# Threshold attention and a low-rank mixer on one core: weight copies and casts of the first five pairs on other engines, and another opening

## The chip, the core and the metric

The kernel runs on one core of a Trainium2 chip. A core has TensorE (PE: matmuls and transposes, with its weight loads shown as PEld), VectorE (DVE), ScalarE (ACT), GpSimd (POOL) and SyncE (SP, which here only issues DMAs). PE writes to PSUM, eight banks of 2 KB in each of 128 partitions; the other tiles lie in SBUF. DMAs are issued here by SP, ACT and POOL. Each engine works through its own instructions in the order in which the program gives them, and semaphores make it wait for the others.

The metric is the device time of one execution in microseconds, the median over runs. Before the change it is 692.33 us (three runs, 691.79 to 692.9).

## The reference

Eight batches of eight heads, 576 positions, 64 columns a head. Attention keeps only the scores that are within tau = 0.02 of their row's largest; its result, 512 columns a position, goes through a mixer of low rank over the positions and a two-layer network over the columns.

```python
scores = scale * np.matmul(q, k.transpose(0, 1, 3, 2))
thresh = np.max(scores, axis=-1, keepdims=True) - tau
scores = np.where(scores >= thresh, scores, -1000000000.0)
attn = np.exp(scores - np.max(scores, axis=-1, keepdims=True))
attn = attn / (np.sum(attn, axis=-1, keepdims=True) + 1e-09)
x = np.matmul(attn, v)                       # then (8, 576, 512)
...
h = x.transpose(0, 2, 1) @ U @ V
u = x + h.transpose(0, 2, 1)
out = u + np.maximum(u @ w_ch1, 0.0) @ w_ch2
```

## The kernel before

The work is cut into 32 pairs of heads, four to a batch. Of a pair, q and k (fp32) are loaded into qkraw, with head 0 and head 1 side by side, and transposed on PE into qkT: `turn_main` for q, `turn_main` for k (four 128x128 transposes each) and `turn_rest` for the last half tiles of both (L625, L638), each followed by a copy on ACT (L631, L644). A pair has 576 rows, which is four and a half tiles of 128; the half tiles of two neighbouring pairs share one step, so two pairs have nine steps. Pairs 0, 2, 4 and so on own the shared step, i = 4.

A step does, for both heads x = 0, 1: scores on PE into a trio of PSUM banks (L696); a copy to SBUF on DVE that also takes the row's extreme (`weigh`, L725, into s_sb and m); the threshold on POOL (L742, into thr); the exponential on ACT (L748, into e_sb); the selection on DVE, which multiplies the exponential by "is over the threshold" and gives the row sum (L755, reads s_sb and e_sb, writes w_ring); a small copy on POOL that doubles the last 64 columns (L766); five transposes on PE (L773); and a copy of these from PSUM to wT_ring or wT4 (`copy_w`, L781). That last copy is on ACT for x = 0 and on DVE for x = 1: `COPIED = (SCA, VEC)`.

`value_tasks` then multiplies the transposed weights by v (L835 to L843), divides by the sums (POOL, L874 for the first four pairs and L901 later), makes a bf16 copy xb of the result (`narrow`, two casts on ACT, L906 and L907), takes it through U and V on PE (L914, L929), adds on DVE (L936), makes a second bf16 copy ub (`narrow_u`, ACT, L943), and transposes that for the network (L951, L959). v itself is split into a high part (`top`, a cast on POOL, L667) and a low part (L660). When the four pairs of a batch are done, `mixer_tasks` runs the two layers on PE (L1024 and L1040 up, L1057 down), spread between the attention steps of later batches. The attention and the mixer of different batches thus lie beside each other, except at the start, where there is no finished batch, and at the end.

The order of all this is written out. Every function call is a `Task` with an engine, a cost, what it depends on and the PSUM banks it needs. A planner outside the kernel has made from them the tuple `ORDER`, which lists the 3,879 tasks in the order in which their instructions are issued to the engines' queues, and `BANK`, which gives the PSUM bank of each. Negative numbers in `ORDER` are `fill` tasks: one matmul on identb into a given bank (L526), without a use for its result. The costs and the due times `DUE` are not read when the kernel is built. `Order.run` walks through the tuple and calls the tasks.

For the opening, the loads of pair 0 go out on three queues: q on SP (three DMAs) and POOL (one), k on ACT (three) and POOL (one). Each is one head's rows of one half of the partitions. The first six pairs after it are loaded by SP alone (`LOADERS`), which also loads v (L587) and sends the outputs; later pairs are loaded by POOL.

Of the kernel before, what the change touches and what calls it, by code (L numbers as in the profile page):

```python
# [68 lines left out]
P = 128  # L69
# [18 lines left out]
COPIED = (SCA, VEC)  # L88
PHASES = (1, 2, 3, 4, 5, 6, 8, 28)
# [4 lines left out]
HIGH = 32  # L94
# [20 lines left out]
class Task:  # L115
# [17 lines left out]
    24, 21, 26, 25, 19, 22, 23, 20, 1, 47, 0, 27, 45, 28, 44, 41, -1, -1, -1, -1, -1, -1, 32, 2, 34, 30, 46, 33, 35,  # L133
    31, 29, 48, -2, -2, 59, 43, 49, 61, 42, 60, 68, 39, -3, -3, -3, -3, -3, 73, 63, 62, 3, 69, 40, 74, 228, 70, 36,
    -8, -8, -8, 71, 75, 225, 77, 87, 64, 224, 56, 82, 72, 226, 89, 37, 227, -6, 52, 76, 88, 57, 50, 53, 231, 78,
    101, 4, 96, 83, 51, 90, 54, 102, 84, 55, 248, 65, 91, 38, 103, -8, -8, 85, 244, 115, 86, 110, 104, 92, 233, 79,
    105, 246, 117, 93, 58, 229, -3, -3, 94, 116, 80, 66, 249, 97, 81, 235, 130, 230, 67, 106, 95, 251, 111, 188,
    124, 247, 132, 112, 236, 118, 232, 98, 131, 107, 119, 245, -7, 108, 125, 189, 113, 99, 252, 109, 144, 120, 139,
    234, 100, 121, 250, 237, 126, 114, 5, 145, 122, 238, 191, 133, 146, 134, 140, 127, 153, 147, 239, 158, 128, 397,
    123, 141, 135, 192, 194, 240, 160, 148, 136, 142, 159, 241, 213, 149, 172, 214, 6, 195, 154, 167, 259, 150, 143,  # L140
    137, 161, 260, 257, 242, 174, 186, 138, 155, 243, 173, 258, -8, 156, 255, 162, 187, 157, 264, 175, 523, 181,
    168, 521, 256, 163, 169, 526, 266, 190, 151, 393, 265, 193, 152, 527, 196, 279, 7, 197, -7, -7, -7, -7, 207,
    402, 182, 164, 273, 524, 278, 267, 198, 176, 183, 396, 165, 274, 184, 166, 170, 129, 185, 275, 199, 280, 268,
    171, 399, -5, -5, 276, 177, 286, 291, 253, 269, 281, 178, 394, 277, 208, 8, 254, 282, 270, 179, 395, 205, 292,
    283, 200, 180, 525, 206, 293, 398, 210, 287, 300, 294, 400, 201, 288, 284, 392, 211, 261, 305, 289, 202, 271,
    306, 295, 262, 290, 272, 307, 296, 308, 318, 301, 313, 309, 285, 302, 319, 203, 297, 212, 405, 320, 204, 263,
    322, 333, 298, 406, 303, 209, 334, 407, 327, 375, 321, 314, 310, 299, 304, 315, 403, 341, 9, 328, 316, 376, 698,
    311, 215, 317, 408, 336, 335, 522, 323, -6, -6, 346, 404, 342, 332, 312, 337, 216, 699, 347, 373, 338, 694, 329,
    217, 324, 348, 343, 350, 401, 330, 360, 218, 349, 528, 344, 325, 361, 529, 363, 339, 378, 374, 695, 326, 362,
    331, 377, 345, 340, 520, 10, 364, 381, 355, 697, 412, 351, 368, 700, 356, 379, 696, 382, 380, 413, 530, 352,  # L150
    365, 414, 383, 693, -8, 531, 416, 409, 353, 426, 384, 369, 415, 354, -8, -8, 219, 535, 385, 427, 532, 370, 366,
    410, 421, 371, 220, 357, 533, 536, 417, 386, 447, 221, 367, 372, 418, 222, 422, 358, 534, 419, 223, 387, 359,
    423, 420, 11, 388, -5, 424, 429, 428, 425, 540, 439, 430, 389, 448, 440, 434, 431, 411, 541, 432, 542, 390, 719,
    441, 391, 554, 543, 544, 713, 555, 444, 449, 442, 545, 549, 567, 435, 433, 537, 445, 550, 562, 556, 569, 546,
    557, 12, 704, 568, 547, 446, 705, 706, 582, 551, 436, 570, 707, 581, 443, 437, 548, 708, 717, 438, 576, 558, -5,
    552, 715, 595, 709, 571, 563, 866, 450, 864, 577, 584, 13, 596, 451, 559, 553, 564, 452, 583, 589, 597, 871,
    565, 453, 560, 566, 720, 454, 561, 716, 458, 572, 455, 870, 604, 459, 598, -4, -4, -4, 456, 14, 651, 609, 457,
    599, 610, 464, 585, 622, 590, 612, 600, 465, 591, 623, 573, 460, 578, 611, 624, 538, 626, 601, 466, 539, 617,
    637, 461, 579, 636, 574, 714, 721, 467, 462, 605, 625, 575, 594, 580, 468, 868, 463, 618, 702, 733, 701, 469,
    627, 631, 723, 613, 652, 722, 632, 639, 703, 592, 734, 644, 633, 606, 586, 593, 619, 649, 15, 737, 470, 747,  # L160
    718, 735, 587, 471, 602, 638, 724, 628, 653, 588, 736, 748, 865, 607, 472, 725, 869, 608, 603, 640, 474, 749,
    473, 645, 614, 760, 475, 738, 671, 750, 739, 755, 761, 620, 742, 762, 615, 476, 616, 775, 763, 646, 764, 478,
    641, 774, 634, 743, 479, 642, 486, 477, 635, 744, 769, 621, 728, 726, 751, 643, 480, 1013, 756, 729, 487, 647,
    867, 481, 629, 770, 482, 1014, 630, 765, 776, 727, 659, 648, 483, 766, 484, 771, 672, 752, 777, 1015, 787, 485,
    16, 778, 660, 782, 1020, 661, 650, 757, 788, 1019, 655, 789, 779, 791, 1016, 740, 803, 790, 656, 745, 710, 741,
    681, 746, 753, 802, 682, 772, 662, 796, 780, 657, 673, 804, 781, 683, 654, 773, 754, 658, 792, 767, 877, 674,
    17, 768, 879, 758, 675, 711, 875, 880, 805, 759, 677, 783, 1186, 878, 676, 876, 797, 488, 678, 730, 810, 815,
    679, 663, 811, 1188, 842, 489, 684, 680, 816, 490, 18, 829, 712, 664, 817, 492, 665, 819, 1192, 830, 666, 491,
    493, 1018, 806, 685, 844, 831, 667, 832, 818, 812, 798, 784, 824, 494, 807, 731, 837, 793, 825, 686, 1017, 813,
    687, 794, 820, 1187, 668, 808, 785, 795, 826, 495, 814, 821, 809, 786, 833, 827, 845, 822, 496, 669, 838, 799,  # L170
    834, 670, 848, 843, 823, 839, 800, 732, 846, 835, 849, 828, 688, 836, 840, 850, 497, 1022, 841, -6, 884, 689,
    801, 1191, 690, 1021, 847, 872, 1189, 885, 1028, 874, 1024, 886, 1029, 1023, 1026, 1025, 898, 887, 873, 852,
    1212, 1027, 899, 691, 851, 921, 853, 888, 854, 855, 922, 1033, 893, 889, 1190, 692, 1211, 923, 894, 1209, 1034,
    499, 900, 890, 881, 1047, 1037, 500, 906, 1035, 895, 882, 891, 911, 1048, 896, 1193, 892, 913, 897, 1036, 901,
    907, 1060, 856, 902, 908, 914, 1042, 915, 1213, 912, 1050, 1062, 903, 501, 1208, 1055, 1061, 916, 857, 1038,
    1206, 909, 858, 904, 502, 910, 1049, 905, 1039, 1210, 1043, 859, 1040, 883, 503, 860, 917, 1069, 1075, 861,
    1207, 506, 1194, 1074, 918, 1030, 1041, 1195, 862, 919, 1199, 1051, 863, 1197, 924, 1200, 1056, 507, 1052, 1064,
    1088, 1077, 1057, 1063, 1076, 1065, 1082, 920, 1198, 1090, 508, 1066, 925, 1031, 1089, 1032, 1201, 1103, 1053,
    1202, 509, 1054, 1102, 1044, 1216, 1091, 1045, 1083, 498, 926, 1058, 927, 1070, 1067, 510, 513, 1110, 1215,
    1059, 1071, 1084, 1046, 928, 1104, 1068, 1214, 514, 929, 1097, 1196, 1078, 1072, 1092, 1115, 1073, 1087, 930,  # L180
    1093, 1105, 1094, 1116, 504, 933, 515, 934, 1117, 516, 935, 1111, 1118, 1085, 517, 931, 936, 1086, 1079, 932,
    1359, 1129, 937, 1080, 1144, 1130, 1081, 1098, 1119, 1095, 1226, 1145, 1106, 1137, 1120, 1107, 1096, 1146, 1124,
    1131, 1227, 938, 518, 1132, 1228, 1217, 1099, 1112, 939, 1138, 1363, 1100, 1221, 1148, 1125, 1360, 1222, 1218,
    1121, 1133, 1229, 1113, 1149, 940, 1235, 1114, 1362, 1101, 1142, 1152, 1358, 1241, 941, 1219, 1230, 1139, 1143,
    1126, 1174, 1236, 1220, 1108, 970, 1240, 1175, 1153, 1248, 1150, 1242, 944, 1109, 1176, 1492, 1231, 971, 1361,
    942, 1154, 1243, 1249, 1237, 1253, 1164, 945, 1357, 1165, 943, 1151, 1232, 1254, 1134, 1127, 1255, 1257, 1122,
    946, 1267, 1256, 1123, 1147, 1128, 1135, 511, 947, 1233, 1268, 1140, 1136, 1238, 1141, 1203, 1234, 948, 1258,
    1262, 1280, 1244, 1364, 1275, 1239, 1155, 1270, 1245, 1263, 1250, 949, 1281, 1166, 1204, 1156, 1205, 1295, 1157,
    1282, 1167, 950, 1264, 1158, 1284, 1269, 1168, 1283, 1246, 1296, 1177, 951, 1159, 1251, 1247, 1271, 1170, 1252,
    1368, 1160, 1171, 1223, 972, 1172, 1161, 1285, 1308, 1488, 973, 1276, 1297, 1369, 1298, 1277, 1173, 1309, 1289,  # L190
# [233 lines left out]
def kernel(  # L424
# [127 lines left out]
    def load_tasks(p, pr):  # L552
# [5 lines left out]
        def one(kind, e, part, to, of, j, deps):  # L558
# [6 lines left out]
            def first(_):  # L565
# [3 lines left out]
                       dma=0.6 if p == 0 and e != POOL else 0.4)  # L569

        lo, hi = slice(0, HB), slice(HB, P)
        loads = {"q": [], "k": [], "v": []}

        by = {"S": SP, "A": SCA, "P": POOL}
        eq, ek, eq3, ek3 = (SP, SCA, POOL, POOL) if p == 0 else \
# [642 lines left out]
```

## Time and profile before

| | us | share of the span |
|---|---|---|
| Median of three runs | 692.33 | |
| The profiled execution, its time | 691.71 | |
| The profiled execution, its span | 689.9 | 100% |
| PE busy | 652.5 | 95% |
| DVE busy | 554.8 | 80% |
| ACT busy | 521.9 | 76% |
| POOL busy | 453.8 | 66% |

The costliest groups, one row each: busy time and mean duration, then how long the engine was idle just before such an instruction and what ended most of that.

```profile
L755 DVE SCALAR_TENSOR_TENSOR w_ring<-s_sb,thr,e_sb 128x576 bf16<-128x576 f32 x288 | 242.0, 863 | 17.9 <-POOL thr L742 5.0
L748 ACT ACTIVATE e_sb<-s_sb,m 128x576 bf16<-128x576 f32 x288 | 217.6, 778 | 36.8 <-DVE s_sb L725 27.7
L725 DVE TENSOR_SCALAR_CACHE_REDUCE s_sb<-trio 128x576 f32<-128x576 f32 x288 | 205.7, 750 | 22.5 <-PE trio L696 18.2
L766 POOL COPY w_ring<-w_ring 128x64 bf16<-128x64 bf16 x288 | 89.6, 328 | 84.4 <-DVE w_ring L755 74.9
```

The granted clock of PE is at full speed in all forty slices of the span. The page's busy time of PE is that of pipelined matmuls whose ends are modelled, so 95% is not PE at its peak. Durations of neighbouring rows on DVE and ACT overlap by some tens of nanoseconds, so the cost of an instruction is read from the distance between two starts where they stand back to back. The share of an engine is a mean over stretches of different kinds; tables by stretch of time say more.

### The profile page before, as it was taken

What the parts mean: (1) busy time and instruction counts of PE and PEld (TensorE: products, weight loads), DVE (VectorE), ACT (ScalarE), POOL (GpSimd) and SP (SyncE); (2) the same over time, 40 slices, a digit from 0 to 9 for tenths busy, and PEclk for the clock granted to TensorE, in tenths of its full rate; (3) what the DMA queues carried; (4) which work ended last, traced back from release to release, by engine and by line L of the source; (5) the groups of instructions that cost most, each with busy time, mean ns of one, the idle gap of its engine ahead of it and who ended that gap; (6) DMA issues with size and microseconds to landing.
All of it is one profiled execution on the core that took longest, in us unless ns stands there. A gap on an engine that the chain in (4) does not pass through costs nothing.

```text
span 689.9 us, 19776 instructions
## 1 busy us (share of the span) xinstructions
PE 652.5 (95%) x7537; PEld 425.6 (62%) x7619; DVE 554.8 (80%) x1469; ACT 521.9 (76%) x1001; POOL 453.8 (66%) x887
## 2 busy tenths in 40 slices
PE   7988899999998999999999999999999999999997
PEld 3655655666666656566667667665666667656543
DVE  5999899889999998997889898899886987772102
ACT  3778779878888968878778788688877886767440
POOL 6566576887688786867887887788567665444020
PEclk9999999999999999999999999999999999999999
DMA  8664252422103132131122213323021321110223
GB/s 146 118 122 90 43 107 66 78 77 66 34 24 94 34 89 59 43 97 41 56 65 60 68 44 97 79 62 86 22 59 41 94 55 24 30 32 2 47 46 77
DMA packets 49503, 44.41 MB, mean 64 GB/s; under 512 B 28672, under 2 KB 40528, under 8 KB 49408
## 3 DMA queue, kind: packets, MB, share of 16 engines
q1 hardware_dynamic: 36320, 23.58, 14.5%
q0 software_dynamic: 12128, 19.22, 12.4%
q8 instruction: 60, 0.98, 0.6%
q10 hardware_dynamic: 960, 0.34, 0.2%
q14 instruction: 35, 0.29, 0.1%
HBM read 37.90 MB, written 9.44 MB: 69 GB/s over the span
## 4 chain that ended last, share of the span: by engine, by line
PE 57%; DVE 16%; ACT 7%; POOL 7%; issue 7%; DMA 4%; SPq 2%; another core or an unknown queue 0%; POOLq 0%; DVEq 0%; ACTq 0%
PE trio L696 12%; DVE w_ring L755 8%; PE trio L1057 8%; PE trio L1024 7%; DVE s_sb L725 6%; PE bank L1057 5%; PE bank L1024 5%; PE trio L773 4%; PE bank L839 3%; PE trio L839 3%; PE bank L773 3%; ACT e_sb L748 3%; POOL qkraw L563 2%; DVE wT_ring L781 2%; POOL x L901 1%
## 5 line engine op out<-in xcount | busy, mean ns | idle before, releaser
L755 DVE SCALAR_TENSOR_TENSOR w_ring<-s_sb,thr,e_sb 128x576 bf16<-128x576 f32 x288 | 242.0, 863 | 17.9 <-POOL thr L742 5.0
L748 ACT ACTIVATE e_sb<-s_sb,m 128x576 bf16<-128x576 f32 x288 | 217.6, 778 | 36.8 <-DVE s_sb L725 27.7
L725 DVE TENSOR_SCALAR_CACHE_REDUCE s_sb<-trio 128x576 f32<-128x576 f32 x288 | 205.7, 750 | 22.5 <-PE trio L696 18.2
L696 PE MATMUL trio<-qkT 64*64 64x288 f32 (+2 forms) x2304 | 160.1, 409 | 3.5 <-DVE wT_ring L781 1.3
L766 POOL COPY w_ring<-w_ring 128x64 bf16<-128x64 bf16 x288 | 89.6, 328 | 84.4 <-DVE w_ring L755 74.9
L773 PEld LDWEIGHTS <-w_ring 128*128 128x128 bf16 x1440 | 91.6, 98 | 48.7 <-issue 15.8
L696 PEld LDWEIGHTS trio<-qkT 64*64 64x64 f32 x2304 | 83.4, 132 | 52.1 <-issue 6.4
L1057 PEld LDWEIGHTS <-R 128*128 128x128 bf16 x576 | 52.6, 98 | 52.9 <-issue 5.6
L773 PE MATMUL trio<-identb,w_ring 128*128 128x128 bf16 x855 | 71.2, 219 | 6.3 <-DVE s_sb L725 3.1
L901 POOL TENSOR_TENSOR x<-x,rec 128x256 f32<-128x256 f32 (+1 forms) x84 | 51.9, 621 | 37.7 <-DVE x L894 33.2
L1024 PEld LDWEIGHTS <-W1b 128*128 128x128 bf16 x512 | 45.6, 98 | 49.2 <-issue 5.8
L563 POOL DMA_DIRECT2D qkraw<-in_q_dram x101 | 67.4, 668 | 9.5 <-PE bank L625 5.5
L742 POOL TENSOR_SCALAR thr<-m 128x2 f32<-128x2 f32 x144 | 44.5, 309 | 43.0 <-DVE s_sb L725 33.6
L1057 PE MATMUL bank<-W2b,R 128*128 128x512 bf16 x268 | 68.3, 379 | 1.8 <-issue 0.5
L563 POOL DMA_DIRECT2D qkraw<-in_k_dram x101 | 67.4, 668 | 3.8 <-issue 2.1
L1057 PE MATMUL trio<-W2b,R 128*128 128x512 bf16 x271 | 68.3, 379 | 1.4 <-ACT R L1014 0.7
L1024 PE MATMUL trio<-uT,W1b 128*128 128x512 bf16 x246 | 62.1, 379 | 3.2 <-DVE s_sb L725 2.3
L1024 PE MATMUL bank<-uT,W1b 128*128 128x512 bf16 x223 | 61.1, 379 | 1.3
L1014 ACT ACTIVATE R<-trio 128x512 bf16<-128x512 f32 x74 | 43.6, 602 | 23.7 <-PE trio L1024 16.8
L839 PEld LDWEIGHTS <-wT_ring 128*128 128x128 bf16 x896 | 55.0, 98 | 7.6 <-issue 4.9
L660 POOL TENSOR_TENSOR vh<-vraw_ring,vh 64x128 bf16<-64x128 f32 (+1 forms) x64 | 54.5, 852 | 2.8
L773 PE MATMUL bank<-identb,w_ring 128*128 128x128 bf16 x585 | 51.1, 219 | 4.1 <-DVE x L936 1.3
(116 smaller groups left out, 1025.3 us busy)
## 6 DMA issues: line engine op xcount, KB each, us to landing
out_dram<-o SPq DMA_DIRECT2D x71, 128.0 KB, 2.4
vraw_ring<-in_v_dram SPq DMA_DIRECT2D x32, 160.0 KB, 3.4
vraw_ring<-in_v_dram SPq DMA_DIRECT2D x32, 128.0 KB, 3.2
qkraw<-in_k_dram POOLq DMA_DIRECT2D x51, 80.0 KB, 2.5
qkraw<-in_q_dram POOLq DMA_DIRECT2D x50, 80.0 KB, 2.7
qkraw<-in_q_dram POOLq DMA_DIRECT2D x51, 64.0 KB, 2.4
qkraw<-in_k_dram POOLq DMA_DIRECT2D x50, 64.0 KB, 2.4
W1b<-in_moe_w_ch_dram POOLq DMA_DIRECT2D x8, 256.0 KB, 4.5
```

What stands on the lines that cost most here:

```text
L563: queue.dma_start(pr.qkraw[part, to, j, :], src[:, j, of, :])
L660: nc.gpsimd.tensor_tensor(out=pr.vh[part, tiles_, :, h, :], in0=raw[part, tiles_], in1=pr.vh[part, tiles_, :, 0, :], op=ALU.subtract)
L696: mm = nc.tensor.matmul(cols[part, lo:hi], a.tT[hs, 0, rows], a.tT[hs, 1, lo:hi], start=True, stop=True)
L725: nc.vector.tensor_scalar(out=s_sb, in0=score_cols(slot, x), scalar1=-scale, scalar2=None, op0=ALU.mult, op1=ALU.min, accum_out=m[:, x:x + 1])
L748: nc.scalar.activation(out=e_sb, in_=s_sb, func=ACT.Exp, bias=m[:, x:x + 1], scale=-1.0)
L755: nc.vector.scalar_tensor_tensor(out=w_sb[:, 0:S], in0=s_sb, scalar=thr_[:, x:x + 1], in1=e_sb, op0=ALU.is_le, op1=ALU.mult, accum_out=pr. ...
L766: nc.gpsimd.tensor_copy(out=w_sb[:, x, S:640], in_=w_sb[:, x, 512:S])
L773: nc.tensor.transpose(ps[:, kt * P:(kt + 1) * P], w_sb[:, kt * P:(kt + 1) * P], identb)
L839: nc.tensor.matmul(av[:, 2 * a + j, :], w, pr.vh[:, kt, j, :, :], start=kt == 0, stop=False)
L901: nc.gpsimd.tensor_tensor(out=x, in0=x, in1=over_sum(part), op=ALU.mult)
L1024: nc.tensor.matmul(bank[t.got[0]], W1b[:, dt, ft * P:(ft + 1) * P], bt.uT[:, dt, :], start=(dt == 0), stop=(dt == 3))
L1057: nc.tensor.matmul(ch, R2[:, ft, lo:lo + P], W2b[:, ft, :], start=(ft == 0), stop=(ft == 15))
```

## The change

It has five parts. Line numbers in the text are those of the kernel before.

First, `FRONT = 5`: in the first five pairs, `copy_w` goes to ACT for both heads in the steps i = 0, 2, 4. For x = 1 that takes 13 copies from DVE. Second, in the same pairs, the casts of `narrow` and `narrow_u` go from ACT to POOL. Third, the opening. For pair 0, k comes first: each half of the partitions is loaded by ACT (head 0) and SP (head 1). q's tile 0 comes apart, by two small loads on POOL, and q's half tile by a load on ACT; q's other tiles are loaded after k, on SP. k is transposed in two tasks of two tiles, one copied by ACT and one by DVE; q's tile 0 is transposed alone and copied by DVE. The first score step waits for q's tile 0, k and the half tiles, and no longer for the rest of q. Fourth, two costs are written differently (`top` 0.72 for 1.1, `copy_w` on DVE 0.404 for 0.42). Fifth, `ORDER` and `BANK` are new throughout, with 3,886 tasks and 23 `fill` entries instead of 43.

```diff
+FRONT = 5
...
 ORDER = (
...
-        for j in range(2):
-            loads["q"].append(one("q", eq, lo, slice(0, 5), slice(0, 5), j, freed))
-            loads["q"].append(one("q", eq3 if j or p else eq, hi, slice(0, 4), slice(5, 9), j, freed))
...
+            k_ = [opening("k", SCA, lo, slice(5, 9), slice(0, 4), one_, 0.5),
+                  opening("k", SP, lo, slice(5, 9), slice(0, 4), two_, 0.5)]
+            k_ += [opening("k", SCA, hi, slice(4, 9), slice(4, 9), one_, 0.6),
+                   opening("k", SP, hi, slice(4, 9), slice(4, 9), two_, 0.6)]
+            loads["q0"] = [opening("q", POOL, lo, one_, one_, both, 0.25),
+                           opening("q", POOL, hi, one_, slice(5, 6), both, 0.25),
+                           opening("q", SCA, lo, slice(4, 5), slice(4, 5), both, 0.25)]
+            loads["k"] = k_
+            for j, e in ((one_, SP), (two_, SP)):
+                loads["q"].append(opening("q", e, lo, slice(1, 4), slice(1, 4), j, 0.4))
+                loads["q"].append(opening("q", e, hi, slice(1, 4), slice(6, 9), j, 0.4))
...
+                def copy_k(_):
+                    nc.scalar.copy(out=pr.tT[:, 1, 0:256], in_=bank[halves[0].got[0]][:, 0:256])
+
+                def copy_k2(_):
+                    nc.vector.tensor_copy(out=pr.tT[:, 1, 256:512], in_=bank[halves[1].got[0]][:, 0:256])
...
+            def copy_q0(_):
+                nc.vector.tensor_copy(out=pr.tT[:, 0, 0:P], in_=bank[q0.got[0]][:, 0:P])
...
-                for name in ("qT", "kT", "qk4T")]
+                for name in (("q0T" if (p, i) == (0, 0) else "qT"), "kT0", "kT", "qk4T")]
...
+            mover = SCA if p < FRONT and i % 2 == 0 else COPIED[x]
...
-            t = add(COPIED[x], 0.42 if COPIED[x] == VEC else 0.575, copy_w, [t], frees=[t])
+            t = add(mover, 0.404 if mover == VEC else 0.575, copy_w, [t], frees=[t])
...
+        front = p < FRONT
+        copy = nc.gpsimd.tensor_copy if front else nc.scalar.copy
...
-            nc.scalar.copy(out=pr.xb[:, 0:4, :], in_=bt.x[:, :, pr.cols])
-            nc.scalar.copy(out=pr.xb[bt.h4, 4, :], in_=bt.x4[bt.h4, pr.cols])
+            copy(out=pr.xb[:, 0:4, :], in_=bt.x[:, :, pr.cols])
+            copy(out=pr.xb[bt.h4, 4, :], in_=bt.x4[bt.h4, pr.cols])
...
-            nc.scalar.copy(out=pr.ub, in_=bt.x[:, :, pr.cols])
+            copy(out=pr.ub, in_=bt.x[:, :, pr.cols])
```

## The prediction

> **What bounds the kernel now.** I read the page's busy times and slices first, then the same by stretches, then what VectorE (DVE) waits for.
>
> ```profile
> PE 652.5 (95%) x7537; PEld 425.6 (62%) x7619; DVE 554.8 (80%) x1469; ACT 521.9 (76%) x1001; POOL 453.8 (66%) x887
> ...
> PE   7988899999998999999999999999999999999997
> ...
> DVE  5999899889999998997889898899886987772102
> ACT  3778779878888968878778788688877886767440
> ```
>
> By the first row TensorE (PE) is the bound at 95%. That is an average. In the slices (17.2 us each) PE is below nine tenths in four of the first six, where DVE mostly shows 9; from there on PE is full, and DVE falls away at the end. The windows sharpen it (per engine: busy us and instructions):
>
> ```profile
> 28.00:68.00 40.00, 35.67 (x589) 24.69 (x587) 39.34 (x110) 31.64 (x62) 25.31 (x58) 1.00 0.54 98
> 68.00:80.00 12.00, 8.72 (x145) 6.97 (x146) 9.07 (x25) 8.69 (x20) 5.35 (x14) 1.00 0.39 63
> 80.00:112.00 32.00, 28.88 (x358) 17.86 (x359) 31.30 (x86) 26.82 (x49) 24.09 (x50) 1.00 0.45 90
> 112.00:135.00 23.00, 22.51 (x268) 15.45 (x270) 20.63 (x58) 19.95 (x40) 18.60 (x36) 1.00 0.35 62
> ```
>
> The third busy column is DVE: 39.3 of 40 us, a gap at 68 to 80, 31.3 of 32, and only after 112 us is PE the fuller one (22.5 of 23). So there are two regimes: up to about 112 us, which is where the first five pairs are worked on, DVE sets the pace, and PE fills part of its time with warm-up matmuls (L526: 39 of 43 stand in the order before the 20th of the 77 score tasks). Afterwards PE does. In 10 to 112 us DVE waits for this:
>
> ```profile
> DVE s_sb L725 <- PE trio L696: 7.7, 5, 6.7
> DVE wT_ring L781 <- ACT wT_ring L781: 1.6, 2, 1.2
> DVE x L936 <- PE trio L929: 1.4, 1, 1.4
> DVE rec L810 <- ACT rec L807: 0.6, 1, 0.6
> DVE w_ring L755 <- POOL thr L742: 0.3, 1, 0.3
> ```
>
> 6.7 of the first row is the start of the kernel itself. What is left is some 5 us in 102: an instruction taken from DVE here is worth nearly its length. In 112 to 560 us it would be worth little by itself.
>
> **The change, part by part.**
>
> *1. Thirteen copies of transposed weights leave DVE for ScalarE (ACT).* Pairs 0, 2, 4 have tiles 0, 2, 4 and pairs 1, 3 have tiles 0, 2 for which the second copy moves: 3x3 + 2x2 = 13. The rows of the two engines (min/median/max ns):
>
> ```profile
> L781 ACT COPY wT_ring<-trio x71: 669/692/755, 22.4 to 628.0; 128x640 bf16<-128x640 bf16 x71
> ...
> L781 DVE COPY wT_ring<-trio x78: 427/485/493, 14.8 to 628.7; 128x640 bf16<-128x640 bf16 x78
> ```
>
> Rows overlap on an engine. On the timeline a DVE copy starts at 42.49 and the next one at 42.89: it costs 0.40, not 0.485. Two ACT copies in a row at 23.00 take 1.29 together: 0.60 each. So DVE gives up 13 x 0.40 = **5.2 us**, and ACT takes on 13 x 0.60 = 7.8 us.
>
> *2. Casts of the first five pairs leave ACT for GpSimd (POOL).* xb is two casts on ACT (medians 618 and 296 ns), ub one (618); less 0.1 overlap each, about 0.72 + 0.52 = 1.24 us a pair, 6.2 us in five. ACT's balance is 7.8 - 6.2 = +1.6 us on the 79.6 us that it is busy in 10 to 112 us; in a front of about 97 us that is 84%. ACT's largest idle there is 7.5 us in which its exponentials (L748) wait for DVE's score row (L725), and no wait of a DVE select (L755) for an exponential is in the list. So I cost ACT at nothing: its idle, and DVE being late itself, hide it. Without that cover the price is rival B. Its lower end is a gain, the 1.6 us of DVE waits for ACT copies, since fewer copies on DVE must follow one on ACT.
>
> POOL has no such cast before. Nearest rows: L667, a cast fp32 to bf16 of 640 columns, median 720 ns, and L766, 64 columns, 238 ns. That is (720 - 238)/576 = 0.84 ns a column, so 0.61 us for 512 columns and 0.29 for 128: xb 0.90, ub 0.61, and 5 x 1.51 = 7.6 us on POOL. POOL is busy 54.8 of 84 us in 28 to 112; with 7.6 more in some 79 us it is at 79%. Behind a cast stand POOL's thresholds (L742) and twin copies (L766), for which DVE and PE wait; today DVE waits 0.3 us for them in the front, which is why I cost the queueing at nothing, with up to 0.6 a cast, 9 us, if each met a threshold that is due. As xb and ub lead to the mixer of batch 0 only through PE work that has the pairs' transposes and scores beside it, their extra 0.1 us each is hidden; uncovered it would be 5 x 0.2 = 1 us.
>
> Here a rule speaks against the change. The Trainium skill (SBUF — State Buffer, Who interferes with whom) says that a VectorE instruction with two SBUF inputs contends with a GpSimd instruction that reads SBUF, and that the later of the two stands fully blocked until the first ends. L755 is such an instruction (s_sb and e_sb), the casts read SBUF. By the rule at its worst each of the 15 casts holds a select for its whole length: 7.6 us, more than the change brings. The rows are far milder. L755 means 863 ns over the kernel and 825 in 10 to 112 us, against 814 for an undisturbed one (its median); 288 x 49 ns = 14.1 us lost, beside 180.7 us of POOL's larger SBUF readers (L660 54.5, L901 51.9, L1076 40.9, L667 26.5, L874 6.8). That is 0.08 us lost for each us of such work, so 7.6 us cost **+0.6**. The ends are 0 and 7.6; I take the row's value. It fits the rule's mechanism, not its worst case.
>
> *3. The opening.* Before, the first score matmuls start 2.6 us after the first transposes (page time 6.02), and DVE starts 1.4 us after that:
>
> ```profile
> 6.05 1.09 PE L625 MATMUL trio<-ident,qkraw 128*128 128x128 f32 x4
> ...
> 7.18 0.59 ACT L631 COPY qkT<-trio 128x512 f32<-128x512 f32 x1 [4.20 <-PE trio L625]
> ...
> 8.62 1.20 PE L696 MATMUL trio<-qkT 64*64 64x288 f32 x16 [0.24 <-ACT qkT L631]
> ```
>
> Nine transposes and three copies in a row on ACT (0.59, 0.27, 0.59) lie in those 2.6 us. Afterwards six transposes come first (q's tile 0, k's four, the shared one) and two engines copy. From the rows: six weight loads at some 0.16, 0.3 until PE's result is out, the last DVE copy about 0.36 (half the columns of a 0.59 ACT copy, for which L870 with 256 columns shows 0.37), 0.1 of hand-over: 1.7 us. That saves 0.9. But the transposes may start later: q's tile 0 comes by POOL's second load, which before was issued at 2.51 and took 3.9 us to land (6.4), against 6.02 now. Net about **-0.6**; ends -1.6 (all of k and q0 there at 5.0) and +0.4. The two copies that DVE gains lie before its first score row, in idle time. A skill rule bears on loading k by two queues: DMA: Bandwidth & Descriptors (Issuing engines are not separate DMA queues) says that several issuing engines only save the issue time. By it the second queue is worth one issue, about 0.7 us in SP's rows; I counted less, since SP's own loads of q now wait behind k's.
>
> SP issues six loads of pair 0 instead of three, but pair 1's values move behind pair 1's q and k: both orders reach pair 1's last load as their 17th issue, at about 12 us. It landed at 16.7, and PE waited 0.6 us for it with the fourth score step queued behind; now that step stands ahead of pair 1's transposes. I count nothing for it.
>
> *4. The whole order and the banks are new.* All 3,886 tasks are re-planned. Counted at equal score tasks, the work ahead of them on PE is within about 1 us of before for most, on DVE 4 to 5 us less from the 16th on. Twenty fillers fall away (43 to 23), 20 x 0.216 = 4.3 us of PE time that stood in waiting; they are the same microseconds and are not added. All remaining costs are equal, so past the front the whole schedule should stand earlier by what the front gained, because PE, full from there on, does the same work from an earlier start.
>
> **Sum.** Span 689.9 - 5.2 + 0.6 - 0.6 = 684.7. The profiled execution took 691.71, 1.8 more than its span, so 686.5. The median of the three runs, 692.33, is 0.6 above that execution: **687.1 us**, 0.75% below. I allow 0.4 for new places where PE waits and say **687.5**.
>
> **The rivals.**
>
> *A. The loads pace the front (no change).* In 62 to 70 us the chain of waits leaves DVE: SP issues values and q/k loads in its fixed order, and the last lands at 70.05:
>
> ```profile
> 62.60 0.55 SPq L587
> 63.20 0.60 SPq L587
> 63.84 1.71 SPq L563
> 65.60 4.31 DMA qkraw<-in_q_dram
> 70.05 0.63 PE bank L625 x4
> ```
>
> If this and later loads hold at their times, DVE's 5.2 us turn into a longer gap at 68 to 80. Against it: SP's loads wait for buffers that earlier work frees, so they move with it. Only some 1 us of opening and later copies would be left: 691.5.
>
> *B. ACT's queue becomes the bound (slower).* Each moved copy waits on PE's transposes, and behind it on ACT's fixed order stand the exponentials, behind these DVE's selects. If each of the 13 delays a select by its own 0.60, that is 7.8 us: 687.5 + 7.8 = 695.3. It decides from (692.3 - 687.5)/13 = 0.37 us a copy. For it: ACT's copies already wait 2.8 us for PE in this stretch. Against it: the idle of ACT above.
>
> *C. The waits of the front go too.* PE waits 3.1 us for qkraw, DVE 1.6 for ACT copies; a better order removes most: 687.5 - 4 = 683.5.
>
> **How the numbers follow.** Forecast 0.52 (685.5 to 690.5, its own range), C 0.18, A 0.13, B 0.17. This kernel's runs can tell about 0.2%, 1.4 us, from nothing. Faster: forecast, C and a little of A, 0.72; same: most of A and of the weaker B, 0.11; slower: 0.17. The range goes from C's 683.5 to 694.0, which takes in part of B and the 7.6 us of port contention up to about 6.
>
> **What would show it.** Right: first scores at about 8.0, 131 DVE copies at L781's successor and 157 on ACT, DVE's busy time in the front still 97% while the score row of the 57th tile (105.8 us now) starts 4 to 6 us earlier, selects there still near 830 ns, and the same distance kept to the end. Wrong: DVE gaps that end at ACT's exponentials (B), PE waits for qkraw grown by several us (A), selects over 900 ns in the front (port), or a lead at 110 us that is gone at 600 (the new order).

## The result, and the profile after

The changed kernel takes 689.8 us (median of ten runs, 689.34 to 690.45); the kernel before, run beside it, takes 691.98 us. The ratio is 0.9967, with a 95% interval from 0.9959 to 0.9976. So it is faster, by 0.33%: the sign and the range of the forecast hold, and the size is less than half of the 4.8 us that were forecast. The profiled execution took 689.98 us with a span of 688.2 us; before it was 689.9 us, so the span lost 1.7 us.

The page of the kernel after, with the same rows as were shown of before (busy us, share of the span, instructions; then busy tenths in 40 slices of 17.2 us), and three of its costliest groups (busy us, mean ns, idle before and what ended it):

```profile
PE 651.1 (95%) x7516; PEld 424.2 (62%) x7599; DVE 562.7 (82%) x1458; ACT 525.7 (76%) x999; POOL 463.0 (67%) x902
...
PE   7988889899999999999999999999998999999997
...
DVE  5999998799999999898899899799888997854001
ACT  3988788777998868987778888878877787767540
...
L818 DVE SCALAR_TENSOR_TENSOR w_ring<-s_sb,thr,e_sb 128x576 bf16<-128x576 f32 x288 | 255.4, 905 | 25.0 <-ACT e_sb L811 10.9
L811 ACT ACTIVATE e_sb<-s_sb,m 128x576 bf16<-128x576 f32 x288 | 216.7, 778 | 30.5 <-DVE w_ring L818 18.3
L788 DVE TENSOR_SCALAR_CACHE_REDUCE s_sb<-trio 128x576 f32<-128x576 f32 x288 | 206.5, 749 | 18.8 <-PE trio L759 13.2
```

Three things are to be seen. DVE has thirteen copies less and is yet busy 7.9 us longer (562.7 for 554.8). The reason stands in the first group, L818, the select that was L755: its mean went from 863 to 905 ns, 12.1 us over the 288. And PE has one new slice below nine tenths far behind the front, the 31st, which covers 516 to 533 us.

The windows of after, over the same stretches as before (us, then busy us of PE, PEld, DVE, ACT and POOL, each with its instructions):

```profile
28.00:68.00 40.00, 36.07 (x608) 25.62 (x603) 39.46 (x110) 35.24 (x67) 29.18 (x64) 1.00 0.55 108
68.00:80.00 12.00, 10.76 (x200) 7.92 (x200) 11.50 (x28) 9.75 (x20) 9.20 (x18) 1.00 0.37 62
80.00:112.00 32.00, 29.30 (x311) 17.23 (x313) 31.76 (x87) 27.44 (x50) 26.39 (x56) 1.00 0.39 80
112.00:135.00 23.00, 21.55 (x273) 14.30 (x275) 18.54 (x49) 16.43 (x32) 18.86 (x36) 1.00 0.40 79
```

and what DVE waits for in 10 to 112 us (us in total, times, longest):

```profile
DVE s_sb L788 <- PE trio L759: 3.0, 2, 2.5
DVE w_ring L818 <- POOL thr L805: 1.2, 3, 0.5
DVE w_ring L818 <- ACT e_sb L811: 0.5, 1, 0.5
```

DVE still paces the front, and the gap at 68 to 80 us is closed. The waits for copies of ACT and for PE's `x` are gone, those for POOL's thresholds have grown from 0.3 to 1.2 us.

How far the kernel is ahead of before, read at the starts of the score rows on DVE (L725 before, L788 after; minus is earlier):

| score row | before, at us | after, us |
|---|---|---|
| 1st | 10.0 | +0.3 |
| 57th | 105.8 | -4.9 |
| 81st | 160.4 | -6.5 |
| 201st | 409.6 | -4.8 |
| 217th | 451.7 | -1.8 |
| 249th | 520.2 | -7.6 |
| 257th | 539.5 | -0.8 |
| last | 613.7 | +0.6 |
| end of the span | 689.9 | -1.7 |

The row order differs, so single rows scatter by some us (the 209th is 9.1 us earlier, the 217th 1.8), and no single row tells where the lead goes. One thing is plain all the same: the 4 to 6 us that the prediction asked for at the 57th row are there, and at the end 1.7 are left. The new gap of PE, the 31st slice, is a place to look for the rest. This is DVE and POOL there:

```profile
521.54 1.34 POOL L565 DMA_DIRECT2D qkraw<-in_k_dram  x2
...
522.12 3.18 DVE L818 SCALAR_TENSOR_TENSOR w_ring<-s_sb,thr,e_sb 128x576 bf16<-128x576 f32 x1
...
522.89 0.63 POOL L966 TENSOR_TENSOR x<-x,rec 128x256 f32<-128x256 f32 x1
...
523.47 1.16 POOL L723 TENSOR_TENSOR vh<-vraw_ring,vh 128x512 bf16<-128x512 f32 x1
...
524.58 1.84 POOL L1144 TENSOR_TENSOR o<-o,x 128x512 f32<-128x512 f32 x1
...
525.23 0.48 DVE L846 COPY wT<-trio 128x640 bf16<-128x640 bf16 x1
...
525.77 2.17 PE L759 MATMUL trio<-qkT 64*64 64x288 f32 x32 [1.30 <-DVE wT L846]
...
531.82 2.41 DVE L818 SCALAR_TENSOR_TENSOR w_ring<-s_sb,thr,e_sb 128x576 bf16<-128x576 f32 x1
...
532.33 1.27 POOL L1144 TENSOR_TENSOR o<-o,x 128x512 f32<-128x512 f32 x1
```

A select takes 3.18 us; the 55 selects of after that have no instruction of POOL beside them have a median of 0.81. Beside it POOL issues two loads and then works through three tensor_tensor instructions without a pause. The DVE copy behind the select is late, and PE waits 1.30 us for it. Ten microseconds on, another select takes 2.41 us. PE is busy 16.87 us of the 20 in 520 to 540, where it was busy 19.82 before (first line after, second before):

```profile
520.00:540.00 20.00, 16.87 (x201) 11.73 (x202) 17.20 (x35) 12.39 (x26) 14.84 (x23) 1.00 0.24 60
...
520.00:540.00 20.00, 19.82 (x225) 13.29 (x224) 14.91 (x39) 15.38 (x32) 15.46 (x26) 1.00 0.17 43
```

No select of before is longer than 1.94 us; after has four above 2.2.

### The profile page after: what moved, and what is told of

It is laid out like the page before. It is cut to its first block, busy times and chain, and to the rows that moved or that the text cites. A ratio compares the mean times of both kernels' runs of the same rounds, so it can differ in the third digit from the quotient of the medians.

```text
span 688.2 us, 19762 instructions
## 1 busy us (share of the span) xinstructions
PE 651.1 (95%) x7516; PEld 424.2 (62%) x7599; DVE 562.7 (82%) x1458; ACT 525.7 (76%) x999; POOL 463.0 (67%) x902
## 3 DMA queue, kind: packets, MB, share of 16 engines
q0 software_dynamic: 12112, 19.13, 12.1%
## 5 line engine op out<-in xcount | busy, mean ns | idle before, releaser
L818 DVE SCALAR_TENSOR_TENSOR w_ring<-s_sb,thr,e_sb 128x576 bf16<-128x576 f32 x288 | 255.4, 905 | 25.0 <-ACT e_sb L811 10.9
L788 DVE TENSOR_SCALAR_CACHE_REDUCE s_sb<-trio 128x576 f32<-128x576 f32 x288 | 206.5, 749 | 18.8 <-PE trio L759 13.2
L829 POOL COPY w_ring<-w_ring 128x64 bf16<-128x64 bf16 x288 | 91.1, 334 | 67.0 <-DVE w_ring L818 57.8
L836 PEld LDWEIGHTS <-w_ring 128*128 128x128 bf16 x1440 | 91.6, 98 | 47.3 <-issue 15.1
L1125 PE MATMUL bank<-W2b,R 128*128 128x512 bf16 x299 | 75.8, 379 | 1.2 <-issue 0.2
L966 POOL TENSOR_TENSOR x<-x,rec 128x256 f32<-128x256 f32 (+1 forms) x84 | 50.6, 605 | 36.1 <-DVE x L959 31.7
L565 POOL DMA_DIRECT2D qkraw<-in_k_dram x100 | 66.6, 667 | 10.1 <-PE bank L655 3.9
L836 PE MATMUL trio<-identb,w_ring 128*128 128x128 bf16 x765 | 65.2, 219 | 6.4 <-DVE s_sb L788 3.3
L1144 POOL TENSOR_TENSOR o<-o,x 128x512 f32<-128x512 f32 x31 | 42.9, 1387 | 35.8 <-ACT o L1141 35.3
L1125 PE MATMUL trio<-W2b,R 128*128 128x512 bf16 x243 | 60.6, 379 | 1.7 <-ACT R L1082 0.9
L836 PE MATMUL bank<-identb,w_ring 128*128 128x128 bf16 x675 | 57.8, 219 | 1.3 <-POOL w_ring L829 0.6
```

The source lines that it names most:

```text
L565: queue.dma_start(pr.qkraw[part, to, j, :], src[:, j, of, :])
L788: nc.vector.tensor_scalar(out=s_sb, in0=score_cols(slot, x), scalar1=-scale, scalar2=None, op0=ALU.mult, op1=ALU.min, accum_out=m[:, x:x + 1])
L818: nc.vector.scalar_tensor_tensor(out=w_sb[:, 0:S], in0=s_sb, scalar=thr_[:, x:x + 1], in1=e_sb, op0=ALU.is_le, op1=ALU.mult, accum_out=pr. ...
L829: nc.gpsimd.tensor_copy(out=w_sb[:, x, S:640], in_=w_sb[:, x, 512:S])
L836: nc.tensor.transpose(ps[:, kt * P:(kt + 1) * P], w_sb[:, kt * P:(kt + 1) * P], identb)
L966: nc.gpsimd.tensor_tensor(out=x, in0=x, in1=over_sum(part), op=ALU.mult)
```

## The experiments

The first theory: the lead is lost at 520 to 540 us because POOL holds up two selects, and casts on POOL do the same in the front. Rivals: the opening costs what the front gains (PE runs slowly there); the end is set by what the new order leaves for PE to do, so that nothing done at 520 us matters; ACT's queue is hurt by the copies. Each run stands beside runs of the kernel before on its own chip (medians 692.18, 691.85, 692.32 and 693.6 us), and is compared by its ratio. A span is that of one profiled execution, and the executions of one kernel differ by 0.1 to 4.8 us, so a difference of two spans is read with the ratios beside it. "After" is the changed kernel, and a select is called held when it takes over 1.3 us.

**e1: more warm-up matmuls in the opening.**

```diff
 ORDER (near its start)
-... -1, -1, -1, -1, 39, ... 32, -3, 66, ...
+... -1, -1, -1, -1, -1, -1, 39, ... 32, -3, -3, 66, ...
```

> The changed kernel with three fill entries given back in the opening: six instead of four before the first transposes, two instead of one before the first scores. Theory cold clock: after the changed kernel's four fillers PE stands 0.7 us before q's tile 0 lands, its matmuls stay slow until about 10.4 us, and the first score step takes 2.2 us instead of 1.2. With PE kept busy from 3.35 us the first score step takes 1.2 us again, DVE's first score row starts at about 9.3 instead of 10.25, and the lead at the 57th score row grows from 4.9 to about 5.8 us; time 688.5 to 689.3 against 689.8, if the late loss stays. Rival, the first step is hidden behind later waits: the score step gets shorter, but DVE's 57th row and the time do not move.

Measured: 689.87 us, ratio 0.9966 (0.9953 to 0.9979), the same as the change. In the opening of after there is this to be seen:

```profile
3.35 1.89 PE L528 MATMUL trio<-identb 128*128 128x512 bf16 x4 [3.35 <-DVE identb L451]
...
5.97 0.44 PE L691 MATMUL trio<-ident,qkraw 128*128 128x128 f32 x1 [0.74 <-DMA qkraw<-in_q_dram]
...
7.88 2.20 PE L759 MATMUL trio<-qkT 64*64 64x288 f32 x16
...
10.25 0.76 DVE L788 TENSOR_SCALAR_CACHE_REDUCE s_sb<-trio 128x576 f32<-128x576 f32 x1 [2.51 <-PE trio L759]
```

The first scores start 0.74 us earlier than before, and sixteen of them take 2.20 us instead of 1.20. With the fillers (L486 there, L717 the scores):

```profile
7.41 1.06 PE L486 MATMUL trio<-identb 128*128 128x512 bf16 x2
8.40 1.58 PE L717 MATMUL trio<-qkT 64*64 64x288 f32 x16
```

The step gets shorter, 1.58 us, and starts 0.5 us later, behind the fillers: the first score row moves from 10.25 to 10.16, where 9.3 was expected. The 57th row stands at 100.8 us for 100.9, and the time is the same, as the rival had it. The opening isn't where the time went.

**e2 and e3: after's order up to its 28th (e2) or 60th (e3) score task, then the tasks and banks of before in before's order.**

> The changed kernel's order up to its 28th score task (about 135 us), from there on the remaining tasks in the order and with the banks of the kernel before. Theory lost by the new order: the lead of 4 to 6 us that the changed kernel has at 135 us reaches the end, since the order that lost it between 505 and 545 us is gone: 686.0 to 687.8. Rival, PE's remaining work sets the end whatever the front does: the lead melts all the same and the time is 689.3 to 690.5, as the changed kernel's. Rival, the two orders do not fit together at the cut: waits there, 690 or more.

> The changed kernel's order up to its 60th score task (about 475 us), the rest in the order and with the banks of the kernel before. Theory lost by the new order: the lead of 3 to 5 us at 475 us is kept, no select of 3 us at 522 us, 687 to 689. Rival, PE's remaining work sets the end: 689.3 to 690.5.

Measured: 691.91 us, ratio 0.9997 (0.9988 to 1.0005), and 692.7 us, 1.0009 (0.9999 to 1.002). Both keep after's lead until the seam and lose it there: e2 goes from 8.8 us ahead at the 89th score row to 0.9 at the 97th, e3 from 1.8 ahead at the 217th to 0.3 at the 225th (after has 5.9 and 3.5 at the 97th and the 225th). The two orders don't fit together at a cut, which costs more than what was to be measured. They are inconclusive on the late loss, except that in e3, where before's order runs at 520 us, PE is busy 19.9 of 20 us there.

**e4: the casts of the first five pairs back on ACT.**

```diff
-        front = p < FRONT
+        front = False
```

> The changed kernel with the xb and ub casts of the first five pairs back on ACT, its order and all else as it is. Theory port: without the 15 casts on POOL the selects of the first 100 us lose about 1.5 to 2 us instead of 4.0 beyond their 0.815 us each. Theory ACT has room: the 6.2 us of casts are hidden on ACT, and the 57th score row starts 1 to 2 us earlier than in the changed kernel; time 688 to 689.5. Rival, ACT then sets the pace, with 13 more copies and the casts: DVE waits for exponentials and copies, the 57th row starts 1 to 4 us later, time 690.5 to 693.

Measured: 689.1 us, ratio 0.9958 (0.9944 to 0.9971). The span is 687.0, 1.2 less than with the casts on POOL; by the ratios it is 0.6 us less, and their intervals overlap. The 57th row is 0.5 us earlier, where 1 to 2 were expected. What a cast does to a select, first in after, then in e4 at the same place:

```profile
68.53 0.61 POOL L974 CAST xb_ring<-x 128x512 bf16<-128x512 f32 x1
69.08 0.28 POOL L975 CAST xb_ring<-x 64x128 bf16<-64x128 f32 x1
...
69.20 1.33 DVE L818 SCALAR_TENSOR_TENSOR w_ring<-s_sb,thr,e_sb 128x576 bf16<-128x576 f32 x1
...
69.32 0.60 POOL L1011 CAST ub<-x 128x512 bf16<-128x512 f32 x1
```

```profile
69.44 0.82 DVE L818 SCALAR_TENSOR_TENSOR w_ring<-s_sb,thr,e_sb 128x576 bf16<-128x576 f32 x1 [0.97 <-ACT e_sb L811]
```

Over the first 100 us, the selects' time above 0.815 us each is 0.84 us before, 4.02 after and 1.49 in e4: 2.5 us are the casts' own in this order (2.1 in the order of before, e6; 1.1 with the copies on DVE, e9 to e10). (In 10 to 112 us a select has a mean of 825 ns before, 875 after, 833 in e4.) ACT, with copies and casts both, is busy 36.7 of 40 us in 28 to 68, and little is late for it: DVE waits 1.0 us for an exponential in 10 to 112 us, 0.5 in after.

**e7: two twins moved ahead in POOL's order.** A twin is the small copy on POOL that doubles the last 64 columns of what the select wrote (L829, L766 in the kernel before), and it can't start before its select has ended. Put right behind its select, it makes POOL wait for the select instead of running norm, low and plus beside it (L966, L723 and L1144 above).

```diff
-... 3436, 3274, 3235, 2453, 3116, 3315, 3244, 3236, 3216, 3316, 3148, ...
+... 3436, 3274, 3275, 3235, 2453, 3116, 3315, 3244, 3236, 3216, 3316, 3148, ...
-... 3269, 3331, 2459, 3123, 3158, 3325, 2447, ...
+... 3269, 3331, 3270, 2459, 3123, 3158, 3325, 2447, ...
```

(3274 and 3269 are the two selects, 3275 and 3270 their twins, which stood some 70 and 20 places later; 3116 is a norm, 3148 a low, 2447 a plus.)

> The changed kernel with two of POOL's twins (the w_ring copies, L829) put earlier in POOL's order, so that POOL waits for the select instead of running norm, low and plus beside it; nothing else is moved. Theory (the lead of the front is kept until 520 us and is lost there because two selects, 3.18 us at 522 and 2.41 us at 532, are held up by POOL's tensor_tensor rows): both selects come down to 0.8 to 1.3 us, PE is busy for over 19 of the 20 us from 520 to 540 instead of 16.9, the lead of 3 to 7 us is still there at the last score row, and the time is 686 to 688. Rival (what is left of PE's work sets the end whatever happens at 520; the new order has that much more left): the selects get short, PE idles somewhere else before the end, and the time is 689 to 690.5.

Measured: 687.79 us, ratio 0.9945 (0.9933 to 0.9957), span 686.1: 2.1 us below after, by two entries of the order. The same place now:

```profile
521.43 1.34 POOL L565 DMA_DIRECT2D qkraw<-in_k_dram  x2
...
522.02 0.81 DVE L818 SCALAR_TENSOR_TENSOR w_ring<-s_sb,thr,e_sb 128x576 bf16<-128x576 f32 x1
...
522.97 0.23 POOL L829 COPY w_ring<-w_ring 128x64 bf16<-128x64 bf16 x1 [0.20 <-DVE w_ring L818]
523.17 0.60 POOL L966 TENSOR_TENSOR x<-x,rec 128x256 f32<-128x256 f32 x1
523.73 0.49 DVE L846 COPY wT<-trio 128x640 bf16<-128x640 bf16 x1 [0.89 <-PE trio L836]
```

The select takes 0.81 us and POOL waited 0.20 for it. The loads on POOL lie beside the select as in after, so they alone don't hold it; with the tensor_tensor rows behind the twin it is free. A twin that comes earlier could also help PE by itself, as PE transposes what it writes; but of PE's waits of after in 519 to 540 us none is for a twin (1.3 us are for the DVE copy, 0.9 and 0.9 for ACT). PE is busy 19.32 of 20 us in 520 to 540. The last score row, 0.6 us late in after, is 1.5 early, where 3 to 7 were expected. The rival that PE's remaining work sets the end is refuted.

**e8: both, and three more twins.** The casts on ACT as in e4, the two twins of e7, and the twins of the selects that took 2.30 us at 255, 2.46 at 353 and 1.8 at 369 moved in the same way.

> The changed kernel with the casts of the first five pairs back on ACT, the same two twins moved, and three more twins moved at selects that took 2.30 us at 255, 2.46 us at 353 and 1.8 us at 369. Theory (port contention): 1.2 us from the casts, 2 to 3 us from the two late selects, up to 1 us from the three others where PE idled for 0.9 to 1.3 of 20 us: 684.5 to 687. Rival (PE's remaining work sets the end): as with the casts on ACT alone, 688.5 to 689.5.

Measured: 683.79 us, ratio 0.9887 (0.9875 to 0.99), span 681.9. It is the fastest of all, and better than was expected. Row by row against e4, whose order it otherwise has, it is 1.2 us earlier from the 145th row on, 2.8 at the 201st and 5.5 at the 257th: about half of what held selects cost in the new order was lost at 255 to 369 us already, which the comparison with before had not shown. No select above 1.7 us is left, and the selects' row is back at the level of before:

```profile
L818 DVE SCALAR_TENSOR_TENSOR w_ring<-s_sb,thr,e_sb 128x576 bf16<-128x576 f32 x288 | 242.6, 861 | 27.2 <-ACT e_sb L811 12.2
```

**e5 and e6: one part alone, in the order of before.** e5 moves only the thirteen copies, e6 only the casts.

```diff
 e5
+            mover = SCA if p < 5 and i % 2 == 0 else COPIED[x]
...
-            t = add(COPIED[x], 0.42 if COPIED[x] == VEC else 0.575, copy_w, [t], frees=[t])
+            t = add(mover, 0.42 if mover == VEC else 0.575, copy_w, [t], frees=[t])
 e6
+        front = p < 5
+        cast = nc.gpsimd.tensor_copy if front else nc.scalar.copy
```

> The kernel before, in its own order and with its own opening, with only the thirteen copies of the first five pairs moved from DVE to ACT. If DVE paces the front, as the prediction has it: the 57th score row stands 4 to 6 us earlier, the selects of the first 100 us stay as before (0.8 us of excess), and the time is 687 to 690 if the old order can use the lead, 691 to 692.5 if it loses it where ACT or POOL are called on in an order made for other durations. Rival (ACT's queue paces the front once it has the copies): the 57th row is less than 2 us earlier, and the time is 692 to 696.

> The kernel before, in its own order, with only the casts of the first five pairs moved from ACT to POOL. Theory (POOL's casts hold up DVE's selects and ACT's time in the front is off the path): the excess of the selects in the first 100 us grows by 1.5 to 3 us, the 57th score row stands 0.5 to 3 us later, and the time is 692 to 694.5. Rival (the 6.2 us that ACT gets free are on the path): the 57th row is 1 us or more earlier and the time 689 to 691.

Measured, e5: 691.85 us, ratio 1.0003 (0.9994 to 1.0013). The copies alone bring nothing beyond the noise, and the 57th row is 1.1 us earlier, not 4 to 6. That row lies where the rival put it (under 2), but not for the rival's reason: in 10 to 112 us DVE's waits for ACT go from 2.2 us to 1.6. The time that DVE gets free turns into idle time, as this window shows (DVE 36.53, before 39.34); what grows are its waits for PE, from 2.4 to 4.0 us without the start, and for POOL, from 0.3 to 1.5.

```profile
28.00:68.00 40.00, 36.13 (x591) 24.89 (x587) 36.53 (x100) 35.36 (x69) 25.50 (x54) 1.00 0.55 103
```

Measured, e6: 696.7 us, ratio 1.008 (1.0061 to 1.0099): the casts alone cost 4.9 us, more than expected. Selects lose 2.1 us more in the first 100 us, and there is a second price that I hadn't sized. In 112 to 150 us PE waits for twins, which stand in POOL's queue behind the casts (before: once, 1.1 us):

```profile
PE trio L773 <- POOL w_ring L766: 2.3, 2, 1.6
```

There may be a third. In the profiled execution of e6 the granted clock of PE is at one half from 91.8 to 95.2 us, right behind several waits of PE for casts and a twin on POOL; none of the other profiles here shows such a dip between the opening and the last 5 us. In the window it reads 0.95 (before 1.00):

```profile
80.00:112.00 32.00, 28.31 (x311) 16.21 (x311) 29.99 (x79) 23.27 (x41) 26.39 (x52) 0.95 0.47 90
```

Up to 1.7 us of this execution's loss of 3.7 us of span may be the clock's; no run separates it.

**e9, e10, e11: the copies put back on DVE in the new order.** e9 also has the casts on ACT, so only the order, banks and opening are new; e10 has the casts on POOL; e11 is e8 with the copies back.

```diff
-            mover = SCA if p < FRONT and i % 2 == 0 else COPIED[x]
+            mover = COPIED[x]
```

> The changed kernel with both moves undone: the thirteen copies back on DVE and the casts of the first five pairs back on ACT, so that only the new order and banks and the new opening are left. Theory A (the order has been made for the lighter DVE; order and copies earn the lead together, since the copies alone in the old order gave 0.5 us): DVE has its 5.2 us back, the lead at the 57th score row shrinks from 5 to under 1.5 us, and the time is 691 to 695. Theory B (the order alone earns it, the copies nothing): the lead at the 57th row is 4 us or more and the time 688 to 690.

> The changed kernel with only the thirteen copies put back on DVE; the casts of the first five pairs stay on POOL. Theory A: 0 to 2 us slower than the run with both undone, since POOL's casts hold up selects there too (692 to 696). Theory B (the casts on POOL are what the new order lives on): faster than the run with both undone by 1 us or more, 687 to 690.

> The fastest kernel so far (casts on ACT, five twins moved, 683.79 us) with the thirteen copies put back on DVE, nothing else. Theory A (the copies are worth what DVE saves, 5.2 us, as long as the lead isn't lost later): 3 to 6 us slower, 687 to 690. Theory B (the copies' place is worth nothing; the selects were all of it): 683.5 to 685.

Measured: e9 691.52 us, ratio 0.9985 (0.9977 to 0.9994); e10 693.09, 1.0007 (0.9998 to 1.0016); e11 686.59, 0.9911 (0.9896 to 0.9925). With the kernels above they make a table of the new order, as spans in us:

| | copies on DVE | copies on ACT | the copies bring |
|---|---|---|---|
| casts on ACT | 690.1 (e9) | 687.0 (e4) | 3.1 |
| casts on POOL | 691.5 (e10) | 688.2 (after) | 3.3 |
| casts on ACT, five twins moved | 684.8 (e11) | 681.9 (e8) | 2.9 |

The copies bring about 3 us in these spans whatever else is done (1.7 to 2.8 by the ratios), the casts on POOL cost 1.2 to 1.4 (0.6 and 1.5), and the five twins bring 5.1 to 5.3 (4.9 and 5.1). In e9 the windows show DVE without any idle time:

```profile
28.00:68.00 40.00, 34.77 (x599) 24.32 (x596) 40.00 (x113) 32.11 (x61) 24.25 (x55) 1.00 0.50 98
...
80.00:112.00 32.00, 29.24 (x329) 17.20 (x327) 32.00 (x90) 27.17 (x51) 23.35 (x50) 1.00 0.44 80
```

So the new order, with the new opening, keeps DVE fed by itself; its 57th row is 1.9 us earlier, and it is then lost again (span 690.1 for 689.9), since its late selects are as long as in after (3.17 and 2.42 us). Theory A holds, but with about 3 us for the copies and not 5.2: the 57th row of e9 keeps 1.9 us of lead where A allowed 1.5, and e11 is 2.8 us slower than e8 where A asked for 3 to 6. e10 stands where A put it.

**e12: the kernel before, with five of its own twins moved ahead** (at selects of 1.3 to 1.94 us).

> The kernel before with five of its own twins moved in POOL's order in the same way, at selects that took 1.70, 1.62, 1.32, 1.82 and 1.94 us (at 218, 241, 277, 360 and 430 us); nothing else. Theory A (a held select costs wherever PE is waiting for weights, in the old order too): the five get down to 0.8 to 1.3 us, 4.2 us of excess less the part that PE covers, and the time is 689 to 691.5. Theory B (the old order has slack at these places, and what the five twins of the new order brought was a loss of the new order's own): within 0.5 us of the kernel before.

Measured: 690.12 us, ratio 0.9951 (0.9934 to 0.9968). Four of the five come down as expected; the one at 277 us stays at 1.31. The profiled execution gains 1.3 us of span; its rows are 1.0 us late up to the 105th, from the opening on, and 1.3 early from the 201st, so the five places bring 2.3 us there. So held selects cost the old order as well, and the remedy is not bound to the change. In the new order five twins bring more, and the five selects had more to lose: 8.1 us above their undisturbed length together, for 4.3 here.

## Why the prediction was right or wrong

**What bounds the kernel** was right: DVE paces the front (39.46 of 40 us busy still), PE the rest. That explains why the sign was right. What it missed is that the rest isn't PE's alone: a single DVE instruction that is 2.4 us late stops PE in the middle of its stretch.

**Step 1, the copies, sized 5.2 us, brought 2 to 3.** The counts were right (131 copies on DVE, 157 on ACT), and so was ACT at nothing: rival B is refuted by e4, where ACT carries the casts too and the kernel gets faster. What failed is "an instruction taken from DVE here is worth nearly its length". From e9 to e4, between the 1st and the 57th score row, DVE's busy time falls by the 5.2 us of the forecast, from 91.6 to 86.4, but its idle time grows from 2.1 to 4.2. Its waits for POOL's thresholds are among what grows (e4: 2.6 us in 10 to 112, e9: none in that list). And in the old order nothing beyond the noise is left (e5).

**Step 2, the casts, sized at +0.6, cost 1.2 to 1.4 us of span in the new order (0.6 and 1.5 by the ratios) and 3.7 in the old one, where the clock may have a part.** Two terms were too small. The casts take 10.1 us on POOL (rows L974 776 ns, L975 604, L1011 640, five each), not 7.6: nine of the fifteen take 0.60 to 0.61 or 0.28 to 0.29, as worked out, but the other six, each of them beside a select, take 0.76 to 1.08. And the twelve casts of the first 100 us, 8.1 us of POOL, cost the selects there 2.5 us (1.1 from e9 to e10), that is 0.14 to 0.3 of their length, where I took 0.08 from a mean over the kernel. That mean hid what the rule says: the Trainium skill (SBUF — State Buffer, Who interferes with whom) has the later instruction fully blocked, and the rows of after show the select at 69.20 ending 0.6 us after the cast L1011, with nothing beside it in e4. By the rows that cast begins 0.12 us after the select, so which of the two was the later one can't be read from their starts. I was right that not each cast meets a select, wrong to let the rule go for a mean that is made of many undisturbed selects and a few that are held entirely.

**Step 3, the opening, sized at -0.6, brought nothing.** The first scores do start at 7.88, as forecast at 8.0. But the step itself takes 2.20 us instead of 1.20. Over the profiles here, four with the old opening have their first score row at 9.59 to 10.61 us, mean 10.15, and nine with the new one (e1 left out) at 9.83 to 10.42, mean 10.21. I took the length of the score step from a trace in which PE had been kept busy by six fillers up to the first transposes, and in which its full clock was granted 1.1 us ahead of that step; in after it is granted at 10.7 us, when the step is over (see the last section).

**Step 4, the new order, taken as "earlier by what the front gained", is the step that failed.** The lead at the 57th row is right, -4.9 us, though made of other parts: -1.9 from the order (e9), -3.5 from the copies (e4), +0.5 from the casts. "The same distance kept to the end" is what the profile refutes: 4.9 us at the 57th row are 1.7 at the end. Of the parts, the copies' -3.5 is still -3.1 there, the casts' +0.5 has become +1.2, and the order's -1.9 has become +0.2: two thirds of the loss are the order's own lead. Two selects that take 3.2 and 2.4 us beside POOL's work at 520 to 540 us cost 2.1 us, as e7 shows, and three more at 255 to 369 us nearly 3, by e8 against e4 (with all five moved, and the casts on ACT, the lead grows on the way instead, from 4.9 us to 8.0). The prediction named this sign, "a lead at 110 us that is gone at 600", but gave it no chance of its own and no size: in the rivals, every loss lay in the front.

**Rival C** was half right: DVE's idle time in the front does fall, from 4.9 to 2.0 us between the first and the 57th row. That pays for the longer selects (3.0 us) there, and so that the forecast at that row came out is luck: two errors of the same size. **Rival A** is not borne out: in the old order (e5) DVE's freed time does become idle time, but the gap at 68 to 80 us gets smaller (DVE busy 10.21 us, before 9.07), and PE's waits for qkraw fall from 3.1 to 1.2 us.

## What to carry to other kernels

When an order is planned anew, its lead has to be followed through the whole span, row by row: a gain of the front can be lost at a few places up to 400 us later, and these are found by the longest instances of a row, not by its mean. Where DVE reads two operands from SBUF and POOL has several instructions of its own ready, put an instruction of POOL that depends on the DVE one ahead of them: at 522 us POOL then waits 0.2 us, and DVE is not held for 2.4; of the ten places tried here, nine got short. And the value of taking work from an engine is not its length but what the order can use; here the same thirteen copies were worth nothing measurable in one order and 2 to 3 us in another.

## What the hardware showed that was not expected

A held select is not always held for one instruction of POOL alone. At 522.12 us it lasted 2.4 us above its own length, across L966 and L723 and into L1144, and the L1144 took 1.84 us instead of 1.27. The ends of held selects follow a pattern: of the 17 in after, 16 end 0.61 to 0.67 us after the end of a tensor_tensor or cast on POOL, as if they did nearly all of their work only then. The starts don't: at 522.12 us the select's row begins 0.77 us ahead of that of L966. Others that start beside such an instruction take 0.81 us, as that at 516.73 us beside an L723, which began 0.04 us later and took 1.06 us where one of its form takes 0.43 elsewhere (74.45 us): there POOL was the one that waited. What decides between the two cases these rows don't show; POOL stood at a DMA issue, a copy or a cast when the selects of 255, 353, 522 and 532 us began. DMA issues alone rarely go with a long select: the 33 selects of after with nothing else of POOL beside them have a median of 0.81 us, like the 55 with nothing at all. Yet the 17th held select (368.65 us, 1.81 us) ends 0.52 us after three such issues, beside the tensor_tensor that follows them, and a select of before (216.34 us, 1.74 us) is like it. That stays open.

In the opening the granted clock reads 1.00 in every window, and so it does in all forty slices of before, and yet the same score matmuls have a median of 684 ns in after's first step and 402 ns before. The 1.00 misleads: the views count the time ahead of the trace's first clock record as full, and that record comes only at 7.5 us before, at 10.7 in after, at 9.2 in e1 and at 9.1 in e4. The score matmuls change with it: ahead of that time they take 680 to 740 ns, behind it 402 to 454, and in e1 and e4 the change falls into the first score step (1.58 and 1.75 us, for 2.20 in after and 1.20 before). With the old opening the first record comes at 6.5 to 8.6 us in four profiles, ahead of the first scores; with the new one at 9.1 to 12.2 in ten, behind their start. That the fillers and the idle stretch of PE (0.74 us in after) set this time is likely, but not shown: e1, with six fillers and no idle stretch, still has 9.2. It also differs between executions of the same opening, which agrees with what the Trainium skill (TensorE: Matmul & The Clock Gate, Part 1) says of a free-running activity window; no row here shows that window.
